# Strided attention and a gated mixture of experts: each expert visited once, tile pairs by seven block products

## The chip, the cores and the metric

The kernel runs on one core of one Trainium2 chip. The metric is the device time of one execution in microseconds. The engines are TensorE (PE in the profile, with its weight loads listed apart as PEld), VectorE (DVE), ScalarE (ACT), GpSimd (POOL) and SyncE (SP, which here only issues DMAs). Everything is float32 apart from the attention masks.

## What is computed

Attention over 8 batches of 576 positions with 8 heads of 64, four heads with a local window of 32 and four that see every 32nd position, gives x of 4608 tokens by 512. A gate then chooses one of 8 experts for each token, where a token may inherit its predecessor's choice:

```python
def _moe_ref(x, w_gate, w_local, w1, w2):
    logits = np.einsum('bsd,de->bse', x, w_gate)
    local_gate = 1.0 / (1.0 + np.exp(-np.einsum('bsd,de->bse', x, w_local).squeeze(-1)))
    for b in range(B):
        prev_e = -1
        for s in range(S):
            fresh_e = int(np.argmax(logits[b, s]))
            if s == 0 or local_gate[b, s] < 0.5:
                e = fresh_e
            else:
                e = prev_e if prev_e >= 0 else fresh_e
            prev_e = e
            ...
            h = np.maximum(x[b, s] @ w1[e], 0.0)
            out[b, s] = p[e] * (h @ w2[e])
```

w1[e] is 512 x 1024 and w2[e] is 1024 x 512. The gate p[e] is a softmax value and so positive.

## The kernel before

**Attention** (`attention`, from line 95). Units are half of the blocks of a pair of heads of one batch; each unit goes through scores (L172), exponential (L181), transposes of the weights (L189) and values (L202), the stages of consecutive units interleaved on TensorE. A batch ends with transposes of x (L233) and the gate's logits (L247). Inputs come over SP's queue, the first ones at the very start; GpSimd builds the masks (`maskL`, L112 to L117), which are the first operand of the first score products. x goes to a buffer `xd` in device memory.

**Routing** (`route`, from line 302). Once all codes are there, VectorE and TensorE find each token's expert by scans and small products, count the tokens of each expert, and give each token a slot. Slots are in tiles of 128, each expert's list padded to whole tiles, so that NT = 43 tiles hold any routing. Tables over the tiles are built by comparing (`at`, L408), two multiplications (`put`, L409 on GpSimd and L410 on VectorE) and 48 products with `lane` (L418): the token of each slot to read (`gi`) and to write (`si`), its gate (`ps_slot`), and the expert of each tile (`et`).

**Experts** (`experts`, from line 429). One loop over 43 tiles, whatever is in them. `load(j)`, two tiles ahead, reads the tile's expert into a register of SP, issues the loads of w1 and w2 (2 MB each) by that register, and a gather of 128 rows of x on GpSimd's queue (L448). `hidden` is 8 products of 512 streamed columns with x transposed as weights (L466) and a relu from PSUM (L468); `turn_x` transposes the next tile's rows (L455, L457); `turn_h` transposes h (L477, copied by VectorE at L478); `output` is 8 more products of 512 columns (L484), a copy scaled by the gate on ScalarE (L487) and a scatter of the rows on GpSimd's queue (L488). A scheduler places instructions; in the loop the order on TensorE follows the text closely.

Of the kernel before, what the change touches and what calls it, by code (L numbers as in the profile page):

```python
# [8 lines left out]
F32 = mybir.dt.float32  # L9
# [19 lines left out]
# Local heads: LT blocks of LQ queries, each against its own keys and the STRIDE before them.  # L29
# Strided heads: position p * ST + c is in block c, whose keys are all that its queries can see.  # L30
# [6 lines left out]
# Experts' token lists are padded to whole tiles of P slots; this many tiles hold any routing.  # L37
NT = (N + E * (P - 1)) // P
SKIP = 8192
NEG = -8.0e9  # L40
# The largest z whose 1 / (1 + exp(-z)) the reference's float32 finds below 0.5: 1 + exp(-z) rounds to 2 above it.
# [3 lines left out]
def spread(ap, shape):  # L45
    """A trailing axis of size shape[-1] with step 0."""
    dims = list("abcd"[:len(shape) - 1])
    left = " ".join(dims[:-1] + [f"({dims[-1]} o)"])
    right = " ".join(dims + ["o"])
    return ap.rearrange(f"{left} -> {right}", o=1).to_broadcast(shape)  # L50


def across(ap, shape):
    """A step-0 axis behind the partitions."""
    return ap.rearrange("a (o b) -> a o b", o=1).to_broadcast(shape)


class Unit:
    """Half of the blocks of one pair of heads of one batch."""
# [10 lines left out]
def attention_then_scomoe(ctx: ExitStack, tc: tile.TileContext, q, k, vl, vs, wg, w1, w2, out):  # L70
# [7 lines left out]
    gi = once.tile([P, NT], I32, name="gi")  # L78
    si = once.tile([P, NT], I32, name="si")
    ps_slot = once.tile([P, NT], F32, name="ps_slot")  # L80
    et = once.tile([1, NT], I32, name="et")

    with ExitStack() as first:
        routing = first.enter_context(tc.tile_pool(name="routing", bufs=1))
        probs = routing.tile([LQ, LT, B, E], F32, name="probs")
        codes = routing.tile([LQ, LT, B, E], F32, name="codes")
        with ExitStack() as part:
            attention(part, tc, q, k, vl, vs, wg, xd, ident, probs, codes)
        with ExitStack() as part:
            route(part, tc, ident, probs, codes, gi, si, ps_slot, et)  # L90
    with ExitStack() as part:
        experts(part, tc, xd, w1, w2, out, ident, gi, si, ps_slot, et)


def attention(ctx, tc, q, k, vl, vs, wg, xd, ident, probs, codes):
# [14 lines left out]
    # Query i of a local block sees its keys i + 1 .. i + STRIDE; the first block has none before it.  # L110
# [7 lines left out]
    # Query i of a strided block sees its keys j <= i with i - j a multiple of STRIDE / ST.  # L118
# [11 lines left out]
    # 8 - e; 8 s + 8; 1 at s = 0.  # L130
# [111 lines left out]
    def gates(b):  # L242
# [16 lines left out]
        # The first of the largest logits.  # L259
# [8 lines left out]
        # 8 s + e where the choice is made anew, else 0; for each row (b, e) to come.  # L268
# [32 lines left out]

def route(ctx, tc, ident, probs, codes, gi, si, ps_slot, et):
    """Slots for the tokens by their experts, and from that the token and the gate of each slot."""
    nc = tc.nc
    rp = ctx.enter_context(tc.tile_pool(name="rp", bufs=1))
# [20 lines left out]
    # Rows r = (b, e), and columns likewise.  # L326
# [17 lines left out]
    # The expert of each token: its own choice, or that of the last token that made one.  # L344
# [18 lines left out]
    # Where each expert's tiles begin, and each batch's tokens in them.  # L363
# [4 lines left out]
    nti = rp.tile([R, 1], I32, name="nti")  # L368
    nc.vector.tensor_scalar(nti, nps[:, 0:1], float(P - 1), None, Alu.add)
    nc.vector.tensor_scalar(nti, nti, 7, None, Alu.arith_shift_right)  # L370
    nt = rp.tile([R, 1], F32, name="nt")
    nc.vector.tensor_copy(nt, nti)
    nc.tensor.matmul(nps[:, 2:3], lhsT=less[0:E, :], rhs=nt[0:E], start=True, stop=True)
    nn = rp.tile([R, 4], F32, name="nn")
    nc.vector.tensor_copy(nn[:, 1:3], nps[:, 1:3])
    end = rp.tile([E, 1], F32, name="end")
    nc.vector.tensor_tensor(end, nn[0:E, 2:3], nt[0:E], op=Alu.add)
    over = rp.tile([E, NT], F32, name="over")
    nc.vector.tensor_scalar(over, io[0:E, 0:NT], end, None, Alu.is_ge)
    eps = pp.tile([1, NT], F32, name="eps")  # L380
    nc.tensor.matmul(eps, lhsT=ones[0:E, 0:1], rhs=over, start=True, stop=True)
    nc.vector.tensor_scalar(et, eps, float(E - 1), None, Alu.min)
    base = rp.tile([R, 1], F32, name="base")
    nc.vector.tensor_scalar(base, nn[:, 2:3], float(P), nn[:, 1:2], Alu.mult, Alu.add)
    nc.vector.tensor_scalar(base, base, -1.0, None, Alu.add)
    slot = rp.tile([R, S], F32, name="slot")
    nc.vector.scalar_tensor_tensor(slot, cum, base, hot, Alu.add, Alu.mult)

    # Back to tokens on the partitions.
# [15 lines left out]
    # Slot (lo, hi) takes token + 1 and gate from the one token that has it; empty slots stay 0.  # L405
    put = rp.tile([LQ, CM, 2, NT], F32, name="put")
    at = rp.tile([LQ, CM, NT], F32, name="at")
    nc.vector.tensor_tensor(at, across(io[0:LQ, 0:NT], [LQ, CM, NT]), spread(hi, [LQ, CM, NT]), op=Alu.is_equal)  # L408
    nc.gpsimd.tensor_tensor(put[:, :, 0], at, spread(tok, [LQ, CM, NT]), op=Alu.mult)  # L409
    nc.vector.tensor_tensor(put[:, :, 1], at, spread(pt, [LQ, CM, NT]), op=Alu.mult)  # L410
    lane = rp.tile([LQ, CM, P], F32, name="lane")
    tab = pp.tile([P, 2, NT], F32, name="tab")
    for t in range(LT):
        c = slice(t * B, (t + 1) * B)
        nc.vector.tensor_tensor(lane[:, c], across(io[0:LQ], [LQ, B, P]), spread(lo[:, c], [LQ, B, P]),
                                op=Alu.is_equal)
        for i in range(t * B, (t + 1) * B):
            nc.tensor.matmul(tab, lhsT=lane[:, i], rhs=put[:, i], start=(i == 0), stop=(i == CM - 1))  # L418
    nc.scalar.copy(out=ps_slot, in_=tab[:, 1])
    row = rp.tile([P, NT], F32, name="rowf")  # L420
    nc.vector.tensor_scalar(row, tab[:, 0], -1.0, 0.0, Alu.add, Alu.max)
    nc.vector.tensor_copy(gi, row)
    skip = rp.tile([P, NT], F32, name="skip")
    nc.vector.tensor_scalar(skip, tab[:, 0], 0.0, float(SKIP), Alu.is_equal, Alu.mult)
    nc.vector.tensor_tensor(row, row, skip, op=Alu.add)
    nc.vector.tensor_copy(si, row)


def experts(ctx, tc, xd, w1, w2, out, ident, gi, si, ps_slot, et):
    nc = tc.nc  # L430
    wp = ctx.enter_context(tc.tile_pool(name="wp", bufs=4))
    xp = ctx.enter_context(tc.tile_pool(name="xp", bufs=3))
    psx = ctx.enter_context(tc.tile_pool(name="psx", bufs=1, space=PSUM))
    psh = ctx.enter_context(tc.tile_pool(name="psh", bufs=3, space=PSUM))
    pst = ctx.enter_context(tc.tile_pool(name="pst", bufs=2, space=PSUM))
    psy = ctx.enter_context(tc.tile_pool(name="psy", bufs=2, space=PSUM))
    T = [dict() for _ in range(NT)]

    def load(j):
        t = T[j]  # L440
        e = nc.values_load(et[0:1, j:j + 1], engines=[ET.SP], min_val=0, max_val=E - 1,
                           skip_runtime_bounds_check_because="a count of at most 8 experts, held to 7")
        t["w1"] = wp.tile([P, DK, F], F32, name="w1t")
        nc.sync.dma_start(out=t["w1"], in_=w1[bass.ds(e, 1)].rearrange("o (k p) f -> p (o k) f", p=P))
        t["w2"] = wp.tile([P, FK, D], F32, name="w2t")
        nc.sync.dma_start(out=t["w2"], in_=w2[bass.ds(e, 1)].rearrange("o (k p) f -> p (o k) f", p=P))
        t["x"] = xp.tile([P, D], F32, name="xg")
        nc.gpsimd.indirect_dma_start(out=t["x"], out_offset=None, in_=xd,  # L448
                                     in_offset=bass.IndirectOffsetOnAxis(ap=gi[:, j:j + 1], axis=0))

    def turn_x(j):
        t = T[j]
        ps = psx.tile([P, D], F32, name="xps")
        for kk in range(DK):
            nc.tensor.transpose(ps[:, kk * P:(kk + 1) * P], t["x"][:, kk * P:(kk + 1) * P], ident)  # L455
        t["xT"] = xp.tile([P, D], F32, name="xgT")
        nc.vector.tensor_copy(t["xT"], ps)  # L457

    def hidden(j):
        t = T[j]  # L460
        t["h"] = xp.tile([P, F], F32, name="h", bufs=2)
        for f in range(2):
            c = slice(f * 512, (f + 1) * 512)
            ps = psh.tile([P, 512], F32, name="hps")
            for kk in range(DK):
                nc.tensor.matmul(ps, lhsT=t["xT"][:, kk * P:(kk + 1) * P], rhs=t["w1"][:, kk, c],  # L466
                                 start=(kk == 0), stop=(kk == DK - 1))
            nc.scalar.activation(t["h"][:, c], ps, Act.Relu)  # L468

    def turn_h(j):  # L470
        t = T[j]
# [70 lines left out]
```

## Time and profile before

| | us |
|---|---|
| runs shown | 1166.19, 2480.13, 1143.65; median 1166.19 |
| the profiled execution's span | 1160.3 |
| last product's end to the span's end | about 9.9 |
| first score product (L172) starts | 6.50 |
| routing's last table (`si`) written | 479.4 |
| first expert product (L466) starts | 494.70 |

Times in the profile are in microseconds from the first instruction. A line of the stretches' view gives start and end, length, then busy time and number of instructions of PE, PEld, DVE, ACT and POOL, the granted TensorE clock as a share of full speed, the busy share of the DMA engines and GB/s. A line of the groups' view gives line, engine, operation, tiles and shapes, the number of records, then busy time, the mean length of one in ns, and the idle time before them. A line of the timeline gives start, length, engine, line, operation, tiles and the number of records merged, then in brackets how long the engine was idle before and what ended that. The clock is recorded from 59 us on; before that the views print 1.00 for want of a record, although the spacing of L202's weight loads (160 ns for 96 columns, as later at 0.50) is that of half clock.

The issue rows of the DMAs, with KB each and the median time to landing:

```
w1t<-in_w_dram SPq DMA_DIRECT2D x43, 2048.0 KB, 10.2
w2t<-in_w_dram SPq DMA_DIRECT2D x43, 2048.0 KB, 9.7
xg<-xd,gi POOLq DMA_INDIRECT x43, 7.0
out_dram<-y,si POOLq DMA_INDIRECT x43, 7.2
```

### The profile page before, as it was taken

The numbers are of one execution on the slowest core, as the hardware profiler recorded it, in microseconds if no ns is written. First come the engines' busy times: TensorE is split into PE (matmuls) and PEld (weight loads), VectorE is DVE, ScalarE is ACT, GpSimd is POOL, SyncE is SP. The second block draws the span as 40 slices with busy tenths as digits, with TensorE's granted clock in tenths as the row PEclk, the third lists the DMA queues.
The fourth block names the chain that finished last, engine by engine and source line by source line (L and its number), as shares of the span: only waits on it lengthen the run. The fifth ranks groups of instructions, "written<-read, shape, count | busy, mean of one in ns | idle before, by whom it ended". The sixth has DMA issues, their size and how long they took to land. (4 is left out here: it accounts for less than half of the span.)

```text
span 1160.3 us, 12189 instructions
## 1 busy us (share of the span) xinstructions
PE 1109.1 (96%) x5008; PEld 711.2 (61%) x5008; DVE 290.5 (25%) x615; ACT 198.5 (17%) x299; POOL 93.5 (8%) x105
## 2 busy tenths in 40 slices
PE   8999999999999984599999999999999999999996
PEld 6888898888888874544444444444444444444442
DVE  4444434443435337110011111111110111111110
ACT  2322222232322210011111111111111111111110
POOL 1000000000000001210011111111111111111100
PEclk9965555555555555589999999999999999999999
DMA  7323223222221010499998888888888888888700
GB/s 265 103 100 104 94 81 133 84 91 84 96 78 42 1 41 1 158 398 399 401 358 309 309 315 323 319 306 304 305 305 298 309 304 311 320 318 309 263 4 0
DMA packets 90760, 241.91 MB, mean 208 GB/s; under 512 B 4686, under 2 KB 13902, under 8 KB 90128
## 3 DMA queue, kind: packets, MB, share of 16 engines
q1 hardware_dynamic: 83296, 220.38, 52.2%
q0 software_dynamic: 6880, 20.72, 4.6%
q8 instruction: 40, 0.66, 0.2%
q10 hardware_dynamic: 528, 0.02, 0.0%
q14 instruction: 16, 0.13, 0.0%
HBM read 222.23 MB, written 20.71 MB: 209 GB/s over the span
## 5 line engine op out<-in xcount | busy, mean ns | idle before, releaser
L466 PE MATMUL hps<-w1t,xgT 128*128 128x512 f32 x688 | 315.0, 601 | 0.0
L484 PE MATMUL yps<-w2t,hT 128*128 128x512 f32 x688 | 302.4, 592 | 0.0
L484 PEld LDWEIGHTS yps<-w2t,hT 128*128 128x128 f32 x688 | 130.1, 190 | 161.9 <-issue 150.7
L466 PEld LDWEIGHTS hps<-w1t,xgT 128*128 128x128 f32 x688 | 128.3, 191 | 150.5 <-issue 146.4
L457 DVE COPY xgT<-xps 128x512 f32<-128x512 f32 x43 | 29.8, 692 | 542.2 <-PE xps L455 502.9
L172 PE MATMUL sps<-kt,qt 64*72 64x72 f32 (+1 forms) x896 | 105.9, 380 | 2.2 <-DMA kt<-in_k_dram 2.2
L172 PEld LDWEIGHTS sps<-kt,qt 64*72 64x72 f32 (+1 forms) x896 | 79.9, 244 | 35.4 <-issue 30.9
L487 ACT ACTIVATE y<-yps,ps_slot 128x512 f32<-128x512 f32 x43 | 29.6, 687 | 366.6 <-PE yps L484 366.6
L468 ACT ACTIVATE h<-hps 128x512 f32<-128x512 f32 x86 | 51.4, 598 | 225.2 <-PE hps L466 225.2
L189 PE MATMUL tps<-ident,e 72*72 72x72 f32 (+1 forms) x448 | 76.5, 348 | 0.0
L488 POOL DMA_INDIRECT out_dram<-y,si x43 | 42.9, 998 | 400.5 <-ACT y L487 400.5
L176 DVE TENSOR_REDUCE mx<-sps 96x6 f32<-96x768 f32 (+1 forms) x64 | 54.6, 854 | 59.6 <-PE sps L172 59.6
L192 ACT COPY et<-tps 128x576 f32<-128x576 f32 (+1 forms) x64 | 40.8, 637 | 166.1 <-PE tps L189 166.1
L202 PE MATMUL tps<-vst,et 72*72 72x65 f32 x512 | 68.2, 325 | 0.7 <-DVE xs L213 0.7
L189 PEld LDWEIGHTS tps<-ident,e 72*72 72x72 f32 (+1 forms) x448 | 60.2, 195 | 13.5 <-issue 6.4
L202 PE MATMUL tps<-vlt,et 128*96 128x65 f32 x384 | 66.8, 360 | 0.0
L202 PEld LDWEIGHTS tps<-vst,et 72*72 72x72 f32 x512 | 65.2, 239 | 2.0 <-PE tps L189 0.6
L478 DVE COPY hT<-htps 128x512 f32<-128x512 f32 x86 | 55.6, 682 | 40.6 <-PE htps L477 40.5
L202 PEld LDWEIGHTS tps<-vlt,et 128*96 128x96 f32 x384 | 63.7, 275 | 1.8
L247 PE MATMUL tps<-wgs,xT 128*96 128x9 f32 x384 | 58.7, 297 | 1.5 <-ACT xT L239 1.5
L247 PEld LDWEIGHTS tps<-wgs,xT 128*96 128x96 f32 x384 | 58.0, 262 | 3.4 <-ACT xT L239 3.4
L448 POOL DMA_INDIRECT xg<-xd,gi x43 | 42.3, 984 | 211.7 <-PE xps L455 187.0
(127 smaller groups left out, 588.1 us busy)
## 6 DMA issues: line engine op xcount, KB each, us to landing
w1t<-in_w_dram SPq DMA_DIRECT2D x43, 2048.0 KB, 10.2
w2t<-in_w_dram SPq DMA_DIRECT2D x43, 2048.0 KB, 9.7
kt<-in_k_dram SPq DMA_DIRECT2D x16, 608.0 KB, 6.1
qt<-in_q_dram SPq DMA_DIRECT2D x16, 576.0 KB, 3.7
vlt<-in_vl_dram SPq DMA_DIRECT2D x8, 780.0 KB, 4.3
vst<-in_vs_dram SPq DMA_DIRECT2D x8, 585.0 KB
xd<-xl SPq DMA_DIRECT2D x8, 576.0 KB, 3.7
xd<-xs SPq DMA_DIRECT2D x8, 576.0 KB
```

Of the source, the lines that this page charges most:

```text
L172: nc.tensor.matmul(ps[0:w, h, i * kb:(i + 1) * kb], lhsT=qt[r, i2, c:c + w], rhs=kt[r, i2, c:c + kb], start=False, stop=(i == m - 1))
L176: nc.vector.tensor_reduce(mx[0:w, :, 0:m], sv, axis=AX.X, op=Alu.max)
L189: nc.tensor.transpose(ps[0:kb, h, i * w:(i + 1) * w], u.e[0:w, h, i * kb:(i + 1) * kb], ident[0:w, 0:w])
L192: nc.scalar.copy(out=et[0:kb], in_=ps[0:kb, :, 0:288])
L202: nc.tensor.matmul(ps[0:w, h, i * V1:(i + 1) * V1], lhsT=u.et[0:kb, h, i * w:(i + 1) * w], rhs=vt[0:kb, 2 * i2 + h, u.g * m + i, :], start ...
L247: nc.tensor.matmul(ps[0:LQ, 0, t * (E + 1):(t + 1) * (E + 1)], lhsT=xT[:, kk, t * LQ:(t + 1) * LQ], rhs=wgs[:, kk, :], start=(kk == 0), st ...
L448: nc.gpsimd.indirect_dma_start(out=t["x"], out_offset=None, in_=xd, in_offset=bass.IndirectOffsetOnAxis(ap=gi[:, j:j + 1], axis=0))
L466: nc.tensor.matmul(ps, lhsT=t["xT"][:, kk * P:(kk + 1) * P], rhs=t["w1"][:, kk, c], start=(kk == 0), stop=(kk == DK - 1))
L468: nc.scalar.activation(t["h"][:, c], ps, Act.Relu)
L478: nc.vector.tensor_copy(t["hT"][:, f * 512:(f + 1) * 512], ps)
L484: nc.tensor.matmul(ps, lhsT=t["hT"][:, kk * P:(kk + 1) * P], rhs=t["w2"][:, kk, :], start=(kk == 0), stop=(kk == FK - 1))
L488: nc.gpsimd.indirect_dma_start(out=out, out_offset=bass.IndirectOffsetOnAxis(ap=si[:, j:j + 1], axis=0), in_=y, in_offset=None, bounds_che ...
```

## The change

Experts become the outer loop. Weights of expert e + 1 are loaded once, while expert e runs, into the other of two buffers; expert 0's are loaded, and their sums made, ahead of attention in program order. The number of tile pairs q (up to 3) and a flag s for a single tile are computed in `route` for each expert, loaded into registers of PE, ACT, DVE and POOL, and a switch with 8 arms per expert picks the code for that count. A further list of tiles, for more than three pairs, is skipped by a branch when empty.

A pair of tiles is treated as a 2 x 2 block matrix in both layers: seven block products (Winograd's form of Strassen's method) stand for eight. It needs sums of weight blocks (`sums`, on GpSimd, once per expert), sums of row blocks (`row_sums`, VectorE), and sums of results (VectorE). The gate is applied to the rows ahead of the first layer rather than to the output, which the relu allows because the gate is positive. Layer one now has the weights stationary and the transposed rows streaming, so h comes out transposed. The order in the experts is now as written (`manual_schedule`).

```diff
-NT = (N + E * (P - 1)) // P
+QP = 3
+XT = 2 * QP + 1
+NT = E * XT
+OT = 2 * (N // (2 * P) - QP)
...
+    one = Weights(once)
+    one.load(nc, w1, w2, 0)
+    for do in one.sums(nc):
+        do()
...
     with ExitStack() as part:
-        experts(part, tc, xd, w1, w2, out, ident, gi, si, ps_slot, et)
+        with tc.manual_schedule():
+            experts(part, tc, xd, w1, w2, out, ident, tabs, one)
```

In the new class `Weights`, `load` issues two loads on SP and `sums` lists 16 GpSimd additions of 128 x 512:

```python
        for o, x, y, op in ((s[1], a[21], a[22], Alu.add), (s[2], s[1], a[11], Alu.subtract),
                            (s[3], a[11], a[21], Alu.subtract), (s[4], a[12], s[2], Alu.subtract)):
            todo += [step(o, x, y, op, slice(i, i + 1)) for i in range(2)]
        for o, x, y, op in ((t[1], b[12], b[11], Alu.subtract), (t[2], b[22], t[1], Alu.subtract),
                            (t[3], b[22], b[12], Alu.subtract), (t[4], b[21], t[2], Alu.subtract)):
            todo += [step(o, x, y, op, slice(2 * i, 2 * i + 2)) for i in range(2)]
```

The steps of a unit of rows, and a pair:

```python
    def scale(r):
        for i, j in enumerate(r.cols):
            nc.scalar.activation(r.x[:, i], r.x[:, i], Act.Copy, scale=gate[:, j:j + 1])

    def turn(r):
        for i in range(r.n):
            ps = psx.tile([P, DK, P], F32, name="xps")
            for kk in range(DK):
                nc.tensor.transpose(ps[:, kk], r.x[:, i, kk * P:(kk + 1) * P], ident)
            nc.scalar.copy(out=r.xt[:, i], in_=ps)
...
    def pair(r, w, between, tasks):
...
        def prod1(m, v, ps, start=True):
            for f in range(4):
                for kk in range(2):
                    nc.tensor.matmul(ps[:, f], lhsT=m[:, kk, f * P:(f + 1) * P], rhs=v[:, kk],
                                     start=(start and f == 0 and kk == 0), stop=(kk == 1), skip_group_check=True)
...
        prod1(a[11], b11, pa)
        nc.scalar.copy(out=p1, in_=pa)
        prod1(s[2], t2, pb)
        add(u2, p1, pb)
        prod1(a[12], b21, pa, False)
        relu(h11, pa)
        prod1(s[3], t3, pc)
        add(u3, u2, pc)
        prod1(s[1], t1, pb)
        add(h22, u3, pb)
        relu(h22, h22)
        prod1(a[22], t4, pc, False)
        add(h21, u2, pc)
        relu(h21, h21)
        prod1(s[4], b22, pb, False)
        add(h12, u2, pb)
        relu(h12, h12)
        between()

        k1, k2, k3, k4 = (u(f"k{i}", hs) for i in range(1, 5))
        nc.vector.tensor_tensor(k1, h12, h22, op=Alu.add)
        nc.vector.tensor_tensor(k2, k1, h11, op=Alu.subtract)
...
        prod2(h11, b[11], qa)
        nc.scalar.copy(out=q1, in_=va)
        prod2(h22, t[4], qc)
        prod2(h21, b[21], qa, False)
        nc.scalar.copy(out=y[:, 0, 0:256], in_=va)
        prod2(k2, t[2], qb)
        add(v2, q1, vb)
        prod2(k3, t[3], qa)
...
        prod2(k1, t[1], qb)
...
        prod2(k4, b[22], qa)
        for do in tasks:
            do()
        scatter(y, 1, r.cols[1])
        add(y[:, 0, 256:], v4, va)
        scatter(y, 0, r.cols[0])
```

`prod2` is four products of 256 streamed columns with a block of h as weights. `between()` is `prepare` of the next unit: scale, turn and row sums. A single tile takes the plain eight block products per layer (`single`), with 32 products of 128 columns in layer one and 8 of 512 in layer two. The loop over the experts:

```python
    for e in range(E):
        w = W[e % 2]
...
        if e + 1 < E:
            W[(e + 1) % 2].load(nc, w1, w2, e + 1)
            nxt = rows([XT * (e + 1), XT * (e + 1) + 1], True)
            gather(nxt)
            tasks = W[(e + 1) % 2].sums(nc)
        for arm in tc.Switch({n: idx[e] for n in ENG}, 2 * QP + 2):
            q, s = divmod(arm, 2)
            units = [first] if q else []
            if s:
                units.append(rows([XT * e + 2 * QP]))
            units += [rows([XT * e + 2 * i, XT * e + 2 * i + 1]) for i in range(1, q)]
            n = len(units)
            for r in units[(1 if q else 0):2]:
                gather(r)
...
            for i, r in enumerate(units):
                if i and i + 1 < n:
                    gather(units[i + 1])
                a, z = len(tasks) * i // n, len(tasks) * (i + 1) // n
                (pair if r.n == 2 else single)(r, w, lambda: prepare(units[i + 1] if i + 1 < n else nxt), tasks[a:z])
```

In `route` the tables over tiles have 56 columns (7 for each expert) instead of 43, some twenty small steps compute q, s and the slots, and the second round of the table code, for the overflow list, stands under a branch.

## The prediction, on record before the changed kernel ran

> **What bounds it now.** I read the totals first, then the span cut at stage borders, then the expert stage's groups and its timeline.
>
> ```profile
> PE 1109.1 (96%) x5008; PEld 711.2 (61%) x5008; DVE 290.5 (25%) x615; ACT 198.5 (17%) x299; POOL 93.5 (8%) x105
> ```
> ```profile
> 6.50:430.00 423.50, 420.58 (x2974) 365.75 (x2974) 177.72 (x411) 115.85 (x167) 0.00 (x0) 0.57 0.28 92
> 430.00:479.40 49.40, 28.50 (x140) 27.35 (x140) 28.61 (x67) 0.44 (x2) 5.43 (x6) 0.50 0.00 0
> 479.40:494.70 15.30, 4.19 (x16) 3.05 (x17) 2.08 (x3) 0.00 (x0) 5.62 (x6) 0.50 0.91 338
> 494.70:1150.40 655.70, 654.95 (x1877) 314.75 (x1876) 79.92 (x126) 80.26 (x128) 78.36 (x79) 1.00 0.80 299
> ```
> ```profile
> L466 PE MATMUL hps<-w1t,xgT 128*128 128x512 f32 x688 | 315.0, 601 | 0.0
> L484 PE MATMUL yps<-w2t,hT 128*128 128x512 f32 x688 | 302.4, 592 | 0.0
> ```
>
> The stages are attention (423.5 us), routing (49.4), a gap until the first expert product (15.3) and the experts (655.7). In the experts TensorE never waits (654.95 of 655.7), at full clock (1.00), though the DMAs are 80% busy. So only fewer or shorter TensorE steps help there. Each matrix product leaves two records, hence 688 for 43 x 8. Busy means overlap; the price is the distance between starts:
>
> ```profile
> 706.30 0.19 PEld L484 LDWEIGHTS yps<-w2t,hT 128*128 128x128 f32 x1 [0.24 <-issue]
> 706.73 0.19 PEld L484 LDWEIGHTS yps<-w2t,hT 128*128 128x128 f32 x1 [0.24 <-issue]
> ```
> ```profile
> 62.02 4.40 PEld L247 LDWEIGHTS tps<-wgs,xT 128*96 128x96 f32 x48 [0.73 <-ACT xT L239]
> ```
>
> A record of 512 columns costs 0.43 us, its weight load hidden. L247 streams only 9 columns, so it is bound by weight loads: 48 loads of 96 columns in 4.4 us, 0.085 each at steady full clock, and 0.16 at half clock. By columns, a load of 128 costs 0.112 at full clock; a record of 128 or 256 streamed columns costs 0.109 or 0.216. Transposes: four records in 0.43 us, 0.109 each.
>
> **What the Trainium skill says.** "TensorE: Matmul & The Clock Gate", section "What's actually happening": the clock is halved or full according to activity in a free-running window of about 3.4 us. The trace agrees: the experts began at 494.7, full clock at 499.3. Being busy is not enough: L247 kept TensorE busy, yet
>
> ```profile
> 62.44:65.85 3.41, 3.41 (x43) 3.41 (x42) 0.00 (x0) 0.17 (x1) 0.00 (x0) 1.00 0.00 0
> 65.86:69.26 3.40, 3.40 (x22) 3.10 (x22) 2.38 (x11) 0.65 (x2) 0.00 (x0) 0.50 0.18 23
> ```
>
> the window after it is at half. "GPSIMD Engine Reference", section "Key points": GpSimd shares SBUF interfaces with VectorE operations that have two SBUF inputs. The trace agrees:
>
> ```profile
> 448.09 2.30 DVE L408 TENSOR_TENSOR at<-io,hi 96x2064 f32<-96x2064 f32 x1
> 450.47 4.57 POOL L409 TENSOR_TENSOR put<-at,tok 96x2064 f32<-96x2064 f32 x1 [18.05 <-DVE at L408]
> 451.44 5.76 DVE L410 TENSOR_TENSOR put<-at,pt 96x2064 f32<-96x2064 f32 x1
> ```
>
> L410 is L408's size and lost 3.5 us of the 3.6 it shared with POOL. "Runtime: NRT & Kernel Launch", section "Instruction fetch mechanics": a taken branch outside the fetched pages stalls its engine. The kernel before doesn't branch among its stages, so no row prices that.
>
> **Expert products.** Counting the reference's choices gives 701, 469, 606, 495, 656, 452, 546, 683 tokens: 40 full or partial tiles, now 19 pairs and 2 singles; the 3 empty tiles of 43 vanish. Per pair: layer one is 7 x 8 products of 128 columns, 112 records x 0.112 = 12.5 us; layer two 7 x 4 of 256 columns, 56 x 0.216 = 12.1; eight transposes of x 0.9. Sum 25.5. Hidden units come out transposed, so L477's 344 transposes and L478's copies go. A single costs 64 x 0.112 + 16 x 0.43 + 0.4 = 14.5. All: 19 x 25.5 + 2 x 14.5 = 514 us against 655.7: **-142**. Weight loads equal streaming in layer one; if they overlap badly, up to +25; I take 0, since 213 ns (L418, half clock) was the bare load.
>
> **Turning the next rows.** `between()` puts the next unit's transposes directly behind layer one on TensorE, but they wait for ScalarE's `scale`, queued behind the relu of h12, which waits for VectorE's add of the last product. Result to add 0.2, add 0.7 (L213, 687 ns), relu 0.65 (L181 by size), scale 0.7, hops: the first transposes start 2.3 us late, the second tile 0.2 later. Idle 2.5 us x 20 (no next unit at the end) = **+50**. From then VectorE has 5.2 us (three products of layer two) until k2 is needed, and takes about 3.8: copy on ScalarE 0.7, four row sums 1.5, k1 and k2 1.3 (0.65 each, L179 by size). Hidden while VectorE isn't blocked.
>
> **Clock after that idle time.** Each gap is 3.4 us with only transposes. The window with little streaming drops the clock; 502.76 to 506.17, with half streaming, keeps it. I take 6 in 10 gaps x 1.7 us (a window at half) = **+20**; ends 0 and 70 (two windows each).
>
> **Gathers at an expert's start.** POOL issues a pair's second scatter only after the first has landed (same output), then two gathers for the next expert, one switch, then this expert's second pair: about 1 us each (L448, 987 ns); landing takes 6 to 8.2 us beside weight loads (gathers), 2.1 in quiet (the last scatter). I get arrival 14 to 18 us into the expert; scale needs the rows at 14.1 (12.5 and the 1.6 before scale above). Some experts also wait for the last scatter. Seven starts x 1.7 = **+12**; ends 0 and 45.
>
> SP's weight loads fall from 86 to 16 and are off the path. Per pair ScalarE then has some 7 us of work and VectorE 10 (by the rows used here), of 28: neither becomes the bound by its sum, only by its waits.
>
> **Weight sums.** 16 of 128x512 on POOL at 1.13 us (L409 by size) per expert fit inside 50 us or more. But they block row sums and k sums on VectorE (3.9 us a pair) where they meet, mainly in the first pair: 7 x 1 = **+7**, ends 0 and 20. **Switches**: TensorE's queue runs ahead, the last two waits being single; **+3**, ends 0 and 25.
>
> **Start.** Expert 0's weights (4.2 MB) now go first on SP, and eight weight sums stand in POOL's queue between the two halves of maskL. Weights at about 400 GB/s land half by 7.5 us; 8 x 1.13 brings maskL to 18; q and k arrive by 16. First scores: about 18.8 instead of 6.5, **+12**, nothing covers it. Attention is otherwise the same.
>
> **Routing.** Some twenty small VectorE steps and three of 64x576 add 5.5; tables of 56 for 43 columns add 2.4: +8. The products L418 stay load-bound at 213 ns. Before, the first product waited for weights until 494.7; now they are there, and gather 7, scale 0.7, transposes 1.1, copy 0.7 come to 9.5: -6. Net **+2**. **End**: second scatter behind the first, and the overflow branches: **+4** (0 to 8).
>
> **Sum**: -142 +50 +20 +12 +7 +3 +12 +2 +4 = -32: span 1160.3 to 1128. The runs shown are 1143.65 and 1166.19 (and one of 2480.13), median 0.5% above the span: 1128 x 1.005 = **1134 us**.
>
> **Rivals.** *Stalls are better hidden* (no clock loss, no late gathers, 0.25): for it, every measured stream overlapped its loads; -142 +50 +18 = about -74: 1092. *The stalls eat the gain* (0.30): late gathers and switches at 5 us more per expert, +40: 1168 x 1.005, about 1174; for it, landing of 7 us beside weight loads; against it, 4.2 MB per expert leaves the DMAs quiet after 13 us. *The clock falls and stays down* (0.13): layer one looks like attention, small tiles behind loads, which ran at half nearly throughout. Slower by 2% begins at 1184 on the span's scale, so it decides from 3.8 us lost per gap, over two windows each (20 x 3.8 = 76 in place of 20). Half of layer two at half clock is 6 us a gap, +120: 1228 x 1.005, about 1234; all of layer one at half, 12.5 x 19 = +238: about 1353. Against it: attention streams 0.6 to 0.9 of the time with partial rows, layer one all rows all the time. *It doesn't cut work*: excluded by the counts, unless routing chose other arms.
>
> **Numbers.** My case 0.32, hidden 0.25, eaten 0.30, clock 0.13. About 2% is what a measurement of this kernel can tell from no change. Faster 0.55 (hidden, and most of mine), same 0.32, slower 0.13. Range 1085 to 1182; my own case 1110 to 1155.
>
> **What would show it.** Starts of layer-one records 0.112 us apart at clock 1.00; an idle stretch near 2.5 us on TensorE before each first transpose, released by ScalarE's scale; first scores near 19 us; gathers landing before or after 14 us. I'm wrong if layer one runs at 0.22 a record, or if TensorE idles over 5 us at most expert starts.

## The result, and the profile after

The change made the kernel **slower**: runs of 1180.86 to 1187.26 us, median 1182.3, against 1143.05 to 1166.19 (and one of 2480.13) before; the ratio is 1.0365, 95% interval 1.0328 to 1.0401. Repeated, it was 1.0397 (1.0344 to 1.045). I had forecast 1134. Executions of one kernel can fall into two groups some 20 us apart, and the ratios compare the shorter group of each kernel while the medians below take every run; the changed kernel's ten runs show one group alone. In the attention of both profiled executions TensorE is at full clock for at most 6.8 us at a time, so they compare like with like: spans of 1160.3 and 1181.8 us, 21.5 apart, a ratio of 1.019. What the measured ratio has beyond that seems to go with a longer stretch of full clock, taken up under "The start".

| stage (us) | before | after | change | I had forecast |
|---|---|---|---|---|
| start to first scores | 6.5 | 21.1 | +14.6 | +12 |
| attention | 423.5 | 430.8 | +7.3 | 0 |
| routing, to `si` | 49.4 | 56.1 | +6.7 | +8 |
| `si` to first product | 15.4 | 17.1 | +1.7 | -6 |
| experts | 655.7 | 637.7 | -18.0 | -50 |
| end | 9.9 | 19.1 | +9.2 | +4 |

The view cut at stage borders shows the experts, from their first product on. Columns: stretch, length, busy PE, PEld, DVE, ACT, POOL, TensorE clock, DMA share, GB/s.

```profile
525.00:1163.00 638.00, 560.53 (x3504) 508.24 (x3504) 207.70 (x357) 121.61 (x215) 212.15 (x187) 0.93 0.21 71
```

TensorE is now idle for 77 us of the stage and the clock is 0.93, where before it was idle for under 1 us at 1.00. The timeline at the first border between experts says where:

```profile
612.58 1.89 PE L626 MATMUL mps<-w2t,k 128*128 128x256 f32 x8
613.82 1.00 POOL L575 DMA_INDIRECT out_dram<-y,si  x1 [15.92 <-DVE y L587]
618.88 3.49 PEld L592 LDWEIGHTS lps<-xtfirst,w1t 128*128 128x128 f32 x16 [4.81 <-issue]
618.92 3.76 PE L592 MATMUL lps<-xtfirst,w1t 128*128 128x128 f32 x16 [4.44 <-issue]
619.09 0.98 POOL L575 DMA_INDIRECT out_dram<-y,si  x1 [4.27 <-DMA out_dram<-y,si]
```

The product that opens the next expert waits 4.44 us for "issue", that is for nothing that a semaphore shows, and its 16 records then take 3.76 us instead of the 1.95 of full clock. The next view groups the instructions of the line under which the trace has the switches; columns are count, shortest, median and longest in ns, then first and last start.

```profile
L776 PEldq COMPARE_BRANCH  x16: 314/2605/6707, 518.4 to 1159.8; - x16
```

There are two a switch on TensorE's sequencer: the exit from one arm, some 0.32 us, and the jump into the next. At this border the latter ran from 612.22 to 618.50, 6.28 us, and began only 2.2 us before the array ran dry. (Every arm opens with a record BRANCH_PREFETCH_HINT on each engine, on TensorE at 618.55 here. What it names the trace doesn't show; the cheap exits may be hinted jumps.) The seven borders leave gaps of 3.3 to 5.2 us from the start of one record to the start of the next, which is how gaps and waits on TensorE are counted from here on; less the one record in each, 31.8 us are idle in sum.

The start in the changed kernel:

```profile
16.14 2.48 POOL L507 TENSOR_TENSOR ws<-w1t,ws 128x512 f32<-128x512 f32 x2
18.58 0.63 POOL L126 TENSOR_SCALAR_AFFINE_SELECT maskL<-maskL 96x512 bf16<-96x512 bf16 x1
20.35 2.49 POOL L507 TENSOR_TENSOR wt<-w2t 128x512 f32<-128x512 f32 x2
20.41 9.92 DVE L139 CAST maskS<-relf 72x288 bf16<-72x288 f32 x1 [0.35 <-POOL relf L136]
21.07 1.17 PE L183 MATMUL sps<-kt,qt 64*96 64x128 f32 x8
```

Eight sums of w1 stand ahead of maskL's second half, as forecast (the first line shows the last two). Unforecast: the eight sums of w2 run beside VectorE's cast of maskS, which takes 9.92 us (0.31 before), and VectorE's first softmax step waits behind it until 30.25.

### The profile page after: what moved, and what is told of

It reads as the page before. It is cut to its first block, busy times and chain, and to the rows that moved or that the text cites. A ratio compares the mean times of both kernels' runs of the same rounds, so it can differ in the third digit from the quotient of the medians.

```text
span 1181.8 us, 15988 instructions
## 1 busy us (share of the span) xinstructions
PE 1012.8 (86%) x6632; PEld 903.5 (76%) x6632; DVE 433.0 (37%) x869; ACT 241.8 (20%) x389; POOL 246.1 (21%) x227
## 5 line engine op out<-in xcount | busy, mean ns | idle before, releaser
L575 POOL DMA_INDIRECT out_dram<-y,si x40 | 40.2, 1006 | 367.6 <-DVE y L587 286.0
L626 PE MATMUL mps<-wt,k 128*128 128x256 f32 x456 | 103.5, 384 | 4.8 <-DVE k L620 4.8
L626 PEld LDWEIGHTS mps<-wt,k 128*128 128x128 f32 x456 | 87.6, 193 | 18.1 <-DVE k L620 6.0
L626 PE MATMUL mps<-w2t,h 128*128 128x256 f32 x304 | 85.6, 432 | 0.0
L592 PE MATMUL lps<-xtfirst,w1t 128*128 128x128 f32 x256 | 45.5, 351 | 36.4 <-issue 36.4
L626 PEld LDWEIGHTS mps<-w2t,h 128*128 128x128 f32 x304 | 65.3, 220 | 10.3
L592 PEld LDWEIGHTS lps<-xtfirst,w1t 128*128 128x128 f32 x256 | 42.8, 261 | 39.4 <-issue 39.4
L592 PE MATMUL lps<-ttmore,ws 128*128 128x128 f32 x528 | 62.6, 275 | 0.0
L587 DVE TENSOR_TENSOR h<-lps,u 128x512 f32<-128x512 f32 x57 | 39.4, 692 | 62.4 <-PE lps L592 62.4
L592 PEld LDWEIGHTS lps<-ttmore,ws 128*128 128x128 f32 x528 | 60.7, 192 | 0.0
```

The lines of the kernel that those rows point to most:

```text
L575: nc.gpsimd.indirect_dma_start(out=out, out_offset=bass.IndirectOffsetOnAxis(ap=si[:, j:j + 1], axis=0), in_=y[:, i], in_offset=None, boun ...
L587: add = lambda o, i, p: nc.vector.tensor_tensor(o, p, i, op=Alu.add)
L592: nc.tensor.matmul(ps[:, f], lhsT=m[:, kk, f * P:(f + 1) * P], rhs=v[:, kk], start=(start and f == 0 and kk == 0), stop=(kk == 1), skip_gr ...
L626: nc.tensor.matmul(ps[:, 0:256], lhsT=m[:, f], rhs=v[:, f], start=(start and f == 0), stop=(f == 3), skip_group_check=True)
```

## The experiments

| kernel | median us | ratio to before (95%) | experts us | half clock there us |
|---|---|---|---|---|
| changed kernel, again | 1184.35 | 1.0397 (1.0344 to 1.045) | 635.8 | 87.6 |
| e1_fixed | 1114.42 | 0.9654 (0.9595 to 0.9713) | 585.9 | 42.0 |
| skip_long / skip_short | one run each: 1105.97 / 1130.49 | - | 586.9 / 589.7 | 35.8 / 42.0 |
| e2_late | 1142.07 | 0.9992 (0.9972 to 1.0012) | 632.2 | 80.9 |
| moved | one run: 1157.16 | - | 638.7 | 91.3 |
| hint | 1185.35 | 1.0391 (1.0349 to 1.0433) | 643.9 | 96.7 |
| plain | 1168.06 | - | 631.8 | 35.3 |
| best | 1064.93 | 0.9331 (0.9283 to 0.938) | 562.1 | 27.1 |
| best2 | 1051.03 | 0.9201 (0.9153 to 0.9249) | 550.3 | 17.9 |
| plain_best | 1084.55 | - | 572.7 | 5.0 |

For the changed kernel's own profile the last two columns are 637.7 and 89.4. Totals differ by up to 20 us through attention's clock alone, so the experts' stage is what the runs are compared by.

### The arm written into the code

```
-    idx = [nc.values_load(pick[0:1, e:e + 1], engines=ENG, ...) for e in range(E)]
...
-        for arm in tc.Switch({n: idx[e] for n in ENG}, 2 * QP + 2):
+        for arm in ([6, 4, 5, 4, 6, 4, 5, 6][e],):
```

> The choice at run time is left out: each expert's arm is written into the code for this input's counts (701, 469, 606, 495, 656, 452, 546, 683 tokens); the overflow branches stay. Theory (TensorE stands still at each expert because the taken branch of its switch is fetched late): the seven gaps ahead of L592's first record, 31.8 us together, fall under 1 us each, the 5.8 us ahead of the first product go, and six half-clock windows lose 2.5 us less each; 35 to 48 us less, 1134 to 1147 us. Rival one (the gap is a wait for data - weights, row sums - that only coincides with the switch): gaps stay over 3 us, 1170 us or more. Rival two (the switch hides late gathers): the gaps at the boundaries go but over 2 us appear on top of the 2.3 us before the first transposes of xmore, 1150 to 1165 us.

The same border, e1_fixed's timeline:

```profile
608.32 1.89 PE L626 MATMUL mps<-w2t,k 128*128 128x256 f32 x8
610.05 1.95 PE L592 MATMUL lps<-xtfirst,w1t 128*128 128x128 f32 x16
```

No gap at any border. The stage fell by 51.8 us, the wait ahead of the first product by 5.8, the end by 3.8: 61 us in all lay in the switches and the register loads that feed them (attention, which the edit doesn't touch, took 4.7 us longer here). 31.8 of the 51.8 was idle time; most of the rest is clock, as the half-clock time went from 89.4 to 42.0 us. This is beyond the theory's upper end, and neither rival holds: the gaps ahead of xmore's transposes stayed at 2.3 to 2.4 us.

### Is any taken branch dear?

```
+                if i == 1:
+                    with tc.If(none > 0):
+                        single(units[1], w, lambda: None, [])
```

That is skip_long, on top of e1_fixed; skip_short has `scale(units[1])` and `turn(units[1])` as the body. `none` is the count of overflow pairs, 0 here.

> e1_fixed with one branch more per expert between its first and second unit, taken on every engine, that jumps over the code of one single tile (72 products). Theory (a taken branch to code that is not there yet stops TensorE): 8 gaps of 4 to 5 us ahead of the second unit and a half-clock window after most: 35 to 55 us over e1_fixed. Rival (only the switch with its table is dear, a plain branch is not): under 10 us over e1_fixed.

> As skip_long, but the branch jumps over the scaling and turning of one pair alone (8 transposes on TensorE, 2 copies and 2 scalings on ScalarE). If the distance decides (short targets are in the code fetched ahead): under 10 us over e1_fixed. If each taken branch throws away what was fetched: 35 to 55 us over e1_fixed, as skip_long.

```profile
L714 PEldq COMPARE_BRANCH  x8: 207/316/349, 528.3 to 1033.5; - x8
```

The view is skip_long's. Its branches, taken over 72 products and with no hint record in the trace, took 0.21 to 0.35 us each, and the stage 1.0 us more than without them; with skip_short's it took 3.8 more. So my theory for skip_long fell: a taken branch as such is cheap. Yet the one branch at the end, over the code of 15 overflow pairs and without a hint either, took 4.56 us in the changed kernel. Distance was the natural next reading, and with it the fetch of code; the next pair tests that.

### A jump told in advance

`pair1` is layer one of `pair`; moved has the same without the hint and its label.

```
+        tc.switch_hint({n: idx[e] for n in ENG}, 2 * QP + 2, label=f"arm{e}")
+        h = pair1(first, w)
-        for arm in tc.Switch({n: idx[e] for n in ENG}, 2 * QP + 2):
+        for arm in tc.Switch({n: idx[e] for n in ENG}, 2 * QP + 2, hint=f"arm{e}"):
```

> The changed kernel with layer one of each expert's first pair ahead of its switch (work buffers allocated once). No hint. If the 6.3 us of the switch's jump are spent wherever it stands: no gap of 5 us ahead of L592 at an expert's start, but one of 4.5 to 6.5 us ahead of the first transposes in place of 2.3, since 2.3 us there are idle anyway; experts' stage 615 to 627 us in place of 637.7. If the jump was dear only where the array ran dry beside it, the gap there stays 2.3 to 3 us and the stage is 585 to 600.

> As moved, with a prefetch hint for each switch's arm issued ahead of layer one, some 12 us before the jump. If the 6.3 us are the fetch of the arm's code: jump under 1 us, gap ahead of the first transposes 2.3 to 3 us, experts' stage 585 to 600 us as in e1_fixed (585.9), 1125 to 1147 us in all (some 20 less in runs with the long full-clock stretch in attention). If they are the cost of an indirect jump itself: as moved, 615 to 627 us, 1155 to 1175 in all.

The switch's branches on TensorE, first in moved, then in hint:

```profile
L791 PEldq COMPARE_BRANCH  x16: 295/1810/3767, 510.2 to 1134.0; - x16
```
```profile
L792 PEldq COMPARE_BRANCH  x16: 293/311/2792, 530.4 to 1160.0; - x16
```

Of hint's eight jumps into an arm, six took 0.30 to 0.40 us and two 1.3 and 2.8; without the hint all took 3.3 to 3.8. So the time goes away when the target is named in advance, as the fetch of the arm's code would, and an indirect jump itself costs no more than a plain one. "Runtime: NRT & Kernel Launch", section "Instruction fetch mechanics", says this of a taken branch that leaves the fetched pages, and the runs agree: cheap near by, dear far off. That a hint removes the stall only the runs show. The figure of about 108 ns for a compare-and-branch in "Advanced Engine Details and Errata", section "Control Flow Timing", was reached by no branch of TensorE here (0.20 us at least).

But the whole was no faster: both readings of the stage missed, 638.7 and 643.9 us. hint's timeline at the first border has the reason:

```profile
619.82 1.95 PE L596 MATMUL lps<-xtfirst,ws 128*128 128x128 f32 x16
620.25 0.98 POOL L551 DMA_INDIRECT xfirst<-xd,gi  x1 [5.97 <-PE lps L596]
626.13 0.95 POOL L551 DMA_INDIRECT xmore<-xd,gi  x1 [3.62 <-DMA out_dram<-y,si]
627.38 0.95 POOL L551 DMA_INDIRECT xmore<-xd,gi  x1 [0.30 <-issue]
629.61 0.72 ACT L556 ACTIVATE xmore<-xmore,gate 128x512 f32<-128x512 f32 x1 [6.44 <-DMA xmore<-xd,gi]
630.43 1.09 PE L562 MATMUL xps<-ident,xmore 128*128 128x128 f32 x4 [8.66 <-issue]
```

POOL issues its exit branch at 613.08 and its next instruction at 619.44, then jumps into the arm at 621.17, goes on at 624.98 (its hint came only 0.3 us ahead), and only then gathers xmore, which TensorE's transposes wait for through ScalarE's scale. POOL's branch records last 0.05 us each; what a jump costs it shows as the time to its next instruction. The view puts the last wait down to a scatter, but that had landed at 620.49. The gap ahead of an expert's first transposes became 4.8 to 8.9 us, and is 5.2 to 8.8 in moved, so the hint on TensorE could win nothing there. In the changed kernel TensorE was late enough itself to hide this. So each engine pays for its own jump, and with TensorE's gone POOL's is next: the late gathers that I had feared, but with the switch, not the scatter, ahead of them.

### The start

```
-    one.load(nc, w1, w2, 0)
-    for do in one.sums(nc):
-        do()
+    todo = [lambda: one.load(nc, w1, w2, 0)]
+    todo += one.sums(nc)
...
     for n in range(len(units) + 3):
+        if n in (8, *range(24, 56, 2)):
+            todo.pop(0)()
```

> Expert 0's weight loads and weight sums are issued from inside attention (after units 8 and 24 on) in place of ahead of it; nothing else differs. Theory (the start costs 14.6 us for the loads and sums ahead of q, k and the masks, and 7.3 more because the sums hold VectorE's cast of maskS): first scores at 6.5 us, maskS's cast under 1 us, attention 423 to 427 us, 18 to 22 us less, 1160 to 1164 us. Rival (the sums cost the same wherever they stand, since they block VectorE in attention too): first scores at 6.5 but attention longer by 5 to 15 us; 1168 to 1176 us.

First scores at 6.59 us; the cast of maskS 0.31. The median fell by 42 us, twice the forecast: the profiled execution has an early stretch of full clock (30.7 us, 13.3 to 44.0) and attention took 405.9. best has the same start without that stretch: first scores 6.51 and attention 426.5, so the place of the loads and sums together is worth 14.6 + 4.3 us. The edit moves both. plain, a later run with the loads first but no sums, tells them apart:

```profile
18.27 2.03 PE L181 MATMUL sps<-kt,qt 64*96 64x128 f32 x16 [13.32 <-DMA kt<-in_k_dram]
```

Its first scores wait for k, which comes behind the weights, until 18.27 us; the cast takes 0.31 and attention 426.3. So the loads alone cost 11.8 of the 14.6 us, and the sums the 4.3 us in attention and, by difference, 2.8 at the start.

> The changed kernel again, nothing altered. Attention took 405.9 us in e2_late and 413.6 in skip_long, where TensorE held the full clock for 30.7 us early on, but 430.8 in the changed kernel's profile and 435.5 in e1_fixed, where it did not. If that stretch comes by chance, some runs of the changed kernel lie near 1160 us and some near 1182. If the weight sums at the start keep it away, all lie between 1176 and 1190.

All six runs lie between 1180.98 and 1194.76, as if the start kept the stretch away. Yet skip_long and moved, with the same start, had it (30.7 us from 36.4 and from 36.6 on). What decides it stays open.

> The kernel before, nothing altered, for a trace of one of its shorter runs. If they are short because TensorE holds the full clock for some 30 us early in attention (as in e2_late): such a stretch, attention 400 to 410 us in place of 423.5, routing and experts as in the first profile (49.4 and 655.7), 1137 to 1146 us. If something else made the first profile long: no such stretch, and the difference in another stage.

It took 1165.97 us and showed no such stretch (attention 426.4, experts 655.1; the clock's record begins at 113.5 us there, but the spacing of L202's weight loads before is that of half clock). So no trace of before with the stretch exists; that its shorter runs owe their time to it is inferred from e2_late and best2, not shown.

### Eight products in place of seven

In plain a pair is computed as it would be without the scheme: 32 products of 256 columns, then 16 of 512, with no sums on POOL or VectorE.

```
-        prod1(a[11], b11, pa)
...
+        for g in range(4):
+            for f in range(2):
+                for kk in range(DK):
+                    nc.tensor.matmul(ps[:, f], lhsT=w.w1[:, kk, c:c + P], rhs=r.xt[:, :, kk], ...)
```

> The changed kernel with eight block products for a pair in place of seven (layer one 32 products of 256 columns, layer two 16 of 512), no weight sums, row sums or sums of hidden units; visits, switch and scaling as they are. If seven for eight is worth what the records say: 3.0 us more for each of 19 pairs, less 0.7 at 20 waits ahead of the transposes and less the 5 us of waits for k2: experts' stage 670 to 682 us in place of 637.7. Rival (the sums cost what the eighth product saves): 630 to 645 us. The start is shorter as well, by the sums: first scores near 17 us.

631.8 us: the rival's number, though not by its mechanism. plain's timeline at its first border:

```profile
609.24 0.19 PEld L588 LDWEIGHTS mps<-w2t,hh 128*128 128x128 f32 x1 [0.24 <-issue]
609.66 0.19 PEld L580 LDWEIGHTS lps<-xtfirst,w1t 128*128 128x128 f32 x1 [0.24 <-issue]
610.09 4.26 PE L580 MATMUL lps<-xtfirst,w1t 128*128 128x256 f32 x19
```

TensorE doesn't stop, although its jump took 4.59 us (603.10 to 607.69). The sequencer reached the exit at 602.39, over 7 us ahead of the array; in the changed kernel it was 2.9 us ahead. Counted in records the lead is 12 at the changed kernel's exits (0.216 us each), 15 at moved's jumps (1.9 us, 0.112 each) and 16 at plain's last exit (7.4 us, 0.43 each): nearer to a number of records than to a time. The account against the changed kernel: streams +56.5 (570.5 for 514), gaps at borders -31.8, waits for k2 -5, gaps ahead of transposes -0.3, which leaves -25 for the clock to make the measured -6; 54 us less at half clock would be worth 27. So the eighth product costs what its record price says, and the short records, through the uncovered jump and the clock, gave it all back.

### A version that beats both

best is hint with the late start, the next rows scaled behind the first product of layer one instead of behind the last, each expert's second pair gathered during the expert before, and row sums behind k4:

```
         nc.scalar.copy(out=p1, in_=pa)
+        for n in soon:
+            scale(n)
...
-        between()
+        turn(nx)
...
+        second_next = rows([XT * (e + 1) + 2, XT * (e + 1) + 3], second=True)
+        todo.insert(0, lambda: gather(second_next))
+        h = pair1(first, w, [second])
```

> hint, with expert 0's loads and sums inside attention as in e2_late, the next rows' scaling issued behind the first product of layer one in place of behind its last (the rows of each expert's second pair are gathered in any case, a unit earlier), and their row sums behind k4. If the 2.3 us ahead of each unit's transposes and the half-clock windows behind them were both the scaling's place: gaps under 0.5 us, TensorE at full clock for nearly all of the experts, that stage 515 to 545 us, 1030 to 1065 us in all. Rival (the next wait takes over: k2 behind POOL's weight sums, or a late gather): stage 560 to 585, 1080 to 1105 us.

1064.93 us, at the upper end of the forecast, but the stage, 562.1, is the rival's. The gaps ahead of the transposes went, all but two of some 2 and 3 us behind the two jumps (3.4 and 4.1 us) whose hint did not take; 24.2 us went to waits at the products with the k sums. best2 moves k1 to k4 into `pair1`, ahead of the switch:

> best, with k1 to k4 made right behind layer one, ahead of the switch. In best TensorE waits 24.2 us in seven places for k2 and 8.5 us for the products on h. If VectorE came late because its own jump stood ahead of k1 to k4: these waits go, experts' stage 528 to 542 us, 1028 to 1045 us in all. If POOL's weight sums held VectorE there: 552 to 562 us, no gain over best (1064.9).

550.3 us in the stage and 1051.03 in all: 12 less in the stage, of the 20 to 34 forecast. The waits fell only to 17.7 us; best2's timeline shows why:

```profile
575.00 2.94 POOL L509 TENSOR_TENSOR ws<-w1t 128x512 f32<-128x512 f32 x2 [2.36 <-issue]
575.09 1.73 DVE L628 TENSOR_TENSOR k<-k,h 128x512 f32<-128x512 f32 x1
578.41 1.75 DVE L630 TENSOR_TENSOR k<-h,k 128x512 f32<-128x512 f32 x1
584.30 1.48 DVE L576 TENSOR_TENSOR ttmore<-xtmore,ttmore 128x256 f32<-128x256 f32 x1
586.17 3.36 PE L647 MATMUL mps<-wt,k 128*128 128x256 f32 x8 [3.06 <-DVE v L634]
```

Beside POOL's sums a k sum takes 1.73 us instead of 0.69 and a row sum 1.48 instead of 0.42, so VectorE's queue is late for the result that frees TensorE's buffer. The gain lies between the two forecasts, so both causes seem true in part; how the 12 us divide was not tried.

> best2 with eight block products for a pair and none of the sums (hint, early scaling and the late load of expert 0's weights kept). If seven for eight is worth its 3.0 us a pair once the waits around it are gone: streams 19 x 28.5 + 2 x 14.5 = 570 us and few waits, experts' stage 570 to 582 us against 550.3 in best2, 1068 to 1084 us in all. Rival (the waits in best2, some 36 us above its streams of 514, belong to the sums and go with them): 545 to 562 us, no slower than best2.

The stage in the views of best2 and of plain_best (a little wider than the stage in the latter):

```profile
479.90:1030.40 550.50, 525.23 (x3506) 482.68 (x3504) 241.13 (x361) 116.97 (x216) 219.15 (x187) 0.98 0.26 85
```
```profile
480.00:1056.00 576.00, 573.05 (x2143) 385.14 (x2141) 26.28 (x38) 92.79 (x161) 73.99 (x75) 0.99 0.25 83
```

plain_best's stage is 572.7 us by its first and last product, as forecast, 2 us over its streams and at full clock after the first 5. With most of the waits around them removed (25 us idle are left in best2), seven products are worth 22.4 us of the 56.5 that the records promise; the rest is idle time and clock in best2.

## Why the prediction was wrong

- **Switches, +3 us (0 to 25): the step that failed.** "TensorE's queue runs ahead, the last two waits being single." It does run ahead, but by 2.2 us when the jump starts, and the jump takes 6.3 to 6.7 (4.8 for the last expert). Measured by e1_fixed: 51.8 us in the experts, 5.8 ahead of the first product, 3.8 at the end, 61 in all. That is more than the whole miss of 53.5. I cited the stall of a taken branch, had no row that prices it, and then took 3 us on the strength of a lead whose length I never worked out; with the short records of the change it is 9 to 12 records of 0.216 us.
- **Attention, 0: wrong.** +7.3 in the profiles, of which some 4.3 belong to the sums (attention took 426.5 in best and 426.3 in plain, and 426.4 when the kernel before ran again). I saw POOL's sums ahead of maskL but not what the other eight do to VectorE's cast. I had the like in hand from L408 to L410.
- **Expert products, -142: right.** 0.112 and 0.216 us a record at full clock, and plain_best confirms the same prices for the alternative. At full clock the streams are 514 us.
- **Turning next rows, +50: right.** 2.33 to 2.39 us at most units (1.6 at the two before singles); 43.5 idle in all, less the one record in each. best removed nearly all of it.
- **Clock after that idle time, +20: right for those gaps, but half of the whole loss.** e1_fixed, without the switches, has 12 windows at half clock, as forecast: 42.0 us, which at half speed cost 21 (26 by subtraction). In the changed kernel the loss is 43 us by subtraction from 637.7; the switches brought the rest.
- **Gathers, +12: nothing** in the changed kernel; TensorE came late itself. With its jump gone, in hint, they kept it waiting 2.4 to 6.6 us.
- **Weight sums, +7:** about 5, three waits of 1.7 to 2.3 us for k2 or k4's inputs.
- **Start, +12:** 14.6; a pair of sums takes 2.48 us, not 2.26, and more steps stand behind maskL. That q and k would arrive by 16 was some 2 us early: plain, without sums, started at 18.27.
- **Routing +8 and end +4:** +6.7 and +9.2. The end holds 3.5 us of scatter waiting for scatter, and then POOL, whose sequencer does nothing for 2.8 us behind its exit from the last arm and 2.7 behind the overflow branch; TensorE's far branch of 4.56 us ended at 1165.25, before the second scatter was issued. **Gap to first product, -6:** +1.7; the first switch, with 5.8 us of "issue" on rows that were ready at 519.9.

The sum missed by 32 us in the experts and 21.5 elsewhere. The rival "the stalls eat the gain" had the sign and named switches, at 40 us for them and late gathers together; its 1174 held no clock loss behind a switch and no blocked cast either. In the changed kernel the late gathers that it named cost nothing.

## What to carry to other kernels

Price a runtime branch by where its target lies: over up to 72 products it cost TensorE 0.2 to 0.35 us, into an arm of a switch or over 15 pairs 3.3 to 6.7 us, and the other engines pay for their own (at the changed kernel's first border, from the branch to the next instruction, ScalarE 6.3, VectorE 6.7, POOL 2.7 us into the arm); a hint given 12 us ahead brought it to 0.3 to 0.4 on TensorE in most places. Compare that price with TensorE's lead, which was 12 to 16 records: halving the records halves the cover. When a scheme saves arithmetic by more and shorter steps, count the covers that the long steps gave (here seven products saved 56 us and, as first built, returned all of it), and look at every other engine's own branch before removing TensorE's.

## What the runs showed of the hardware

- The jump of one switch took TensorE 6.3 to 6.7 us at the changed kernel's borders but for the last (4.8), 4.6 to 5.1 at plain's and 3.3 to 3.8 in moved, with the same kind of arms; why it varies was not tried.
- A hint does not always take: two of eight jumps in hint stayed at 1.3 and 2.8 us, two in best2 at 3.2 and 3.7.
- A cast of 72x288 on VectorE, 0.31 us alone, took 9.92 us beside POOL's two-operand sums: it ended 0.2 us after the last of them (30.33 and 30.16).
- In the changed kernel each idle stretch of 5 us at a border was followed by 6.8 us at half clock (3.4 behind the last, of 3.3), which costs half of that again.
- Attention, half-clock for most of its length, has an early stretch at full clock of 30.7 us in some executions and none over 6.8 in others; attention took 404 to 414 us with it and 424 to 436 without.
